# Batch 1 of a retention-then-MLP kernel: its last 256 tokens in 64-token chunks at two stops, its first 256 with 64-column states, and more half-width up products

## The chip, the cores and the metric

The kernel runs on one core of one Trainium2 chip. The metric is the device time of one execution in microseconds (us). A core has a matrix engine (TensorE, PE in the profile; its weight loads are PEld), a vector engine (DVE), a scalar engine (ACT), a general engine (POOL) and a queue engine (SP) that issues most transfers. Each runs its own list of instructions in order and waits on semaphores for the others.

## The reference

For 8 batches and 8 heads, with 576 tokens and 64 features a head, linear attention with a decay per head is computed; the heads are put side by side (512 features a token), and every one of the 4608 tokens goes through a two-layer network with a gate.

```python
scores = scale * np.matmul(q, k.transpose(0, 1, 3, 2))
gamma = 1.0 - 2.0 ** (-5.0 - np.arange(H, dtype=np.float32))
Dmat = np.where(rel >= 0, gamma[:, None, None] ** rel[None, :, :], 0.0)   # rel = query position - key position
ret = scores * Dmat[None, :, :, :]
attn_out = np.matmul(ret, v)
x = attn_out.transpose(0, 2, 1, 3).reshape(B * S, H * D)
h = x @ w_in                          # 512 -> 2048
g = h * (1.0 / (1.0 + np.exp(-beta * h)))
out = g @ w_out                       # 2048 -> 512
```

## The kernel before, in words

**Blocks.** The first 512 tokens of each batch are one block, and the last 64 tokens of all batches together are a ninth block. Each block is attended, which leaves a tile `xT` (features on partitions, tokens along the free axis); then 16 calls of `up` (one for each group of 128 hidden features: four matmuls over the 512 input features, and one ACT instruction that writes the gated result to `gT`) and 16 calls of `down` (four calls of four feature groups for each 128 tokens). Operands are bf16, sums are f32 in PSUM.

**Attention in chunks.** The decay is folded into q and v, so that a chunk needs a plain triangle mask. A chunk's output is (scores within the chunk) times v, plus q times a state, the running sum of the products of k and v over the earlier chunks. The kernel has three ways of doing it. Batch 0 uses functions with the prefix `s_`. Batch 1 uses four chunks of 128 tokens, numbered i = 4 to 7, each in these steps: `t_k` turns k with four transposes; `a_sc` makes scores and masks them on DVE; `a_st` adds the chunk's k by v to the state, as four 128x128 products of which only the two diagonal 64x64 blocks are of use, and copies these blocks to `sbds`; `a_O` multiplies the masked scores by v; `a_cross` adds q times the state (four products over the block-diagonal `sbds`); `a_x` copies the result to `xT`. `second(i)` runs `a_O`, `a_cross` and `a_x` for chunks i and i+1, and then `a_st(i + 1)`. Batches 2 to 7 use eight chunks of 64 tokens with 64x64 tiles of the array: `d_st(u, x)` makes the state products of four chunks and returns `chain`, which adds them up on DVE one after the other and copies each sum to bf16 in `sbq` (on ACT); `d_sc` makes scores and returns `masks` (two DVE instructions for each half); `d_out` makes outputs, first the products with v, then the products with the states in two passes, the second of which waits for a tiny DVE instruction, the fence; its `evict` copies four banks to `xT`. In these batches the heads in the second half of each tile are put in another order (`turned`, `head_of`), so that two products that run side by side write different banks.

**Order of work.** It is written out by hand. `fill` is the list of calls of `up` and `down` in order; `streams` holds the attention steps with keys, and `merged` puts a step before the entry of `fill` whose index reaches its key. `d0` is the index of block 0's first `down`, `u1` that of block 1's first `up`, and `base[m]` that of a later block, from which keys of later loads and attention steps are counted. Block 1's first ten feature groups are done in two halves of 256 tokens (`up(1, fo, 0, 2)`, then `up(1, fo, 2, 2)`), so that they can start on chunks 4 and 5 while chunks 6 and 7 are still attended. The steps of chunks 6 and 7 are spread between the half calls: `t_k(6)` ahead of the first one, `t_k(7)` behind it, and `a_sc(6)`, `a_sc(7)`, `a_st(6)` and `second(6)` further on, three half calls ahead of the second halves.

**PSUM.** There are eight banks: three with tag `mm`, two with `O`, two with `sc`, one with `st`. A new tile of a tag takes the oldest bank of that tag, and its first writer waits for the last reader of the old one.

Of the kernel before, what the change touches and what calls it, by code (L numbers as in the profile page):

```python
# [19 lines left out]
def kernel(  # L20
# [46 lines left out]
    NQ = 6  # L67
    E = CB
    XB = 2
    QB = 2  # L70
    HT = MB // 2
    VB = 4
    q_tiles, kv_tiles = {}, {}
# [208 lines left out]
    def pre_q(b, n):  # L282

        if n == 0:
            batch[b] = dict(qs=sb.tile([P, CB, H, D], BF16, name="qs", tag="qs", bufs=2),
                            qT=sb.tile([P, CB, HP, P], BF16, name="qT", tag="qT", bufs=2))
        if b < 2:
            hs, cs = slice(n // 2 * HP, (n // 2 + 1) * HP), slice(n % 2 * 2, n % 2 * 2 + 2)
            e = nc.vector
        else:  # L290
            if n % 2:
                return
            cs = slice(n, n + 2)
            for to, hs in turned:
                nc.gpsimd.tensor_tensor(batch[b]["qs"][:, cs, to], q_tiles[b][:, hs, cs].rearrange("p h i d -> p i h d"),  # L295
                                        gq[:, cs, hs].unsqueeze(3).to_broadcast([P, 2, len(range(H)[hs]), D]), ALU.mult)
            return
        e.tensor_tensor(batch[b]["qs"][:, cs, hs], q_tiles[b][:, hs, cs].rearrange("p h i d -> p i h d"),
                        gq[:, cs, hs].unsqueeze(3).to_broadcast([P, cs.stop - cs.start, hs.stop - hs.start, D]),
                        ALU.mult)  # L300

    def pre(i, js=(0, 1)):

# [57 lines left out]
    def q_cols(i, r, p):  # L361

        b, c = seq[i]
        if b is None:
            return live[i]["qkT"][r, 0, p, :], lambda o: o
        return (batch[b]["qT"][r, :, p, c * PC:(c + 1) * PC], lambda o: o.rearrange("k (i s) -> k i s", i=CB))
# [31 lines left out]
    def a_cross(i):  # L398

        b, c = seq[i]  # L400
        if c == 0:
            return
        for p in range(HP):
            rhs, view = q_cols(i, slice(0, P), p)
            nc.tensor.matmul(view(O_of(i, p)), sbds[c - 1][:, p, :], rhs, start=False, stop=True, skip_group_check=True)

    def a_O(i):

        b, c = seq[i]
        L = live[i]  # L410
        new_O(i)
        R, vn = L["R"], L["vn"]
        for j, p in [(n % 2, n // 2) for n in range(H)]:
            nc.tensor.matmul(O_of(i, p)[j * D:(j + 1) * D], vn[:, 2 * p + j, :], R[:, j, p, :],
                             start=opens(i, p), stop=c == 0, skip_group_check=True)

    def a_x(i):
# [9 lines left out]
    def a_st(i):  # L427

        b, c = seq[i]
        if b is None:  # L430
            return
        L = live[i]
        if c == 0:
            state_ps[b] = psum.tile([P, HP, P], F32, name="st", tag="st", bufs=1)
        st = state_ps[b]
        for p in range(HP):
            nc.tensor.matmul(st[:, p, :], heads(L["kn"], p), heads(L["vn"], p),
                             start=(c == 0 and p == 0), stop=True, skip_group_check=True)
        for j in range(2):
            r, cols = slice(j * D, (j + 1) * D), slice(j * D, (j + 1) * D)  # L440
            e = nc.vector.tensor_copy if i in (CB + 2, CB + 3) else nc.scalar.copy
            if c < CB - 1:
                e(sbds[c][r, :, cols], st[r, :, cols])
                continue
            e(ends[b][r, :2], st[r, :2, cols])
            e(ends[b][(1 - j) * D:(2 - j) * D, 2:], st[r, 2:, cols])

    spread = [(0, 0), (1, 1), (0, 1), (1, 0)]

# [104 lines left out]
    def after(later, earlier):  # L554
        tc.add_manual_dep(later.ins, earlier.ins.name, mybir.DependencyInfo(mybir.DependencyClass.Sync, mybir.DependencyReason.DATA))

    def d_sc(u):

        R = [sb.tile([P, 2, 2, HP, TL], BF16, name="R", tag="R", bufs=4) for _ in range(2)]
        sc = {}  # L560
        for x in range(2):
            for j in range(2):
                sc[x, j] = psum.tile([P, 2, HP, TL], F32, name="sc", tag="O" if x else "sc", bufs=2)
            for cl in range(2):
                for p in range(HP):
                    for j, hh in spread:
                        c = 4 * x + 2 * cl + hh
                        nc.tensor.matmul(columns(u, sc[x, j][half(hh), cl, p, :]), piece(u, c)["kT"][half(j), p, half(hh)],  # L568
                                         q_of(u, c, j, p), start=cl == 0 and p == 0, stop=True, skip_group_check=True)
        mask = tri[1 if u == B else 0][:].unsqueeze(1).to_broadcast([P, 2 * HP, TL])  # L570
        batch.setdefault(u, {})["R"] = R

        def masks(x):
            for j in range(2):
                nc.vector.tensor_tensor(R[x][:, j].rearrange("k c p q -> k (c p) q"),  # L575
                                        sc[x, j].rearrange("k c p q -> k (c p) q"), mask, ALU.mult)
        return masks

    def d_st(u, x):

        S = [psum.tile([P, 2, HP, D], F32, name="st", tag=t, bufs=n) for t, n in (("st", 1), ("mm", 3))]
        for cl in range(2):
            for p in range(HP):
                for hh, j in spread:
                    L = piece(u, 4 * x + 2 * cl + hh)
                    nc.tensor.matmul(S[hh][half(j), cl, p, :], L["kn"][half(hh), 2 * p + j, :],  # L586
                                     L["vn"][half(hh), head_of(u, p, j), :], start=cl == 0 and p == 0, stop=True,
                                     skip_group_check=True)

        def chain():  # L590
            for c in range(4 * x, 4 * x + 4):
                new, add = sums[c % 2], S[c % 2][:, c // 2 % 2]
                if c:
                    nc.vector.tensor_tensor(new[:], add, sums[(c - 1) % 2][:], ALU.add)  # L594
                else:
                    nc.vector.tensor_copy(new[:], add)
                nc.scalar.copy((sbq[c] if c < NC - 1 else ends[u])[:], new[:])  # L597
        return chain

    def d_out(u):  # L600
# [42 lines left out]
        return lambda: cross(1), evict  # L643


    gts = {}

    def up(m, fo, c0=0, cn=CB):
# [32 lines left out]
    def down(m, ms, f0, fn=4, n0=0, nn=d_model):  # L681

        gT = gts[m]
        if f0 == 0:
            pos_[ms] = psum.tile([P, d_model], F32, name="po", tag="mm" if m or ms < 3 else "st", bufs=3 if m or ms < 3 else 1)
        po = pos_[ms]
        for fo in range(f0, f0 + fn):
            parts = ((0, nn),) if m or fo < 5 else ((0, nn // 2), (nn // 2, nn))
            for x, y in parts:
                nc.tensor.matmul(po[:, x:y], gT[:, fo, ms, :], w_out_sb[:, fo, n0 + x:n0 + y],  # L690
                                 start=(fo == 0), stop=(fo == FO - 1), skip_group_check=m == 0)
        if f0 + fn < FO:
            return
        if m not in ots:
            ots[m] = stage.tile([P, MB // P, d_model], F32, name="ot", tag="wt", bufs=4)
        ot = ots[m][:, ms, n0:n0 + nn]
        (nc.scalar.copy if m == 0 else nc.vector.tensor_copy)(ot, po[:, :nn])  # L697
        if m < B:
            rows = out[m * S:m * S + MB].rearrange("(s i) n -> s i n", i=CB)
            if m < 2:  # L700
                held.append((rows[:, ms, n0:n0 + nn], ot))
            else:
                nc.sync.dma_start(rows[:, ms, n0:n0 + nn], ot)
        else:
            for x in range(2):
                r0 = (2 * ms + x) * S + MB
                nc.sync.dma_start(out[r0:r0 + TL, n0:n0 + nn], ot[x * TL:(x + 1) * TL])
# [102 lines left out]
    fill += [F(down_rows, n) for n in range(3)]  # L810
    fill += [F(down, 0, 3, 0)] + [F(down, 0, ms, f0) for f0 in (4, 8) for ms in range(4)] + [F(down, 0, ms, 12) for ms in (3, 0, 1, 2)]

    u1 = len(fill)
    fill += [F(up, 1, fo, 2 * x, 2) for x in range(2) for fo in range(10)]
    fill += [F(up, 1, fo) for fo in range(10, FO)]
    fill += [F(down, 1, ms, f0) for ms in range(MB // P) for f0 in range(0, FO, 4)]
    base = {1: u1 + 10}
    for n, m in enumerate(blocks[2:], 2):
        base[n] = len(fill)
        fill += [F(up, m, fo) for fo in range(FO)]  # L820
# [2 lines left out]
    fill += [F(down, blocks[-1], MB // P - 1, 0, FO, n0, nn) for n0, nn in ((0, 384), (384, 128))]  # L823

    def second(i):
        for f in (a_O, a_cross, a_x):
            f(i)
            f(i + 1)
        a_st(i + 1)

    def triangles():
        nc.gpsimd.memset(causal, 1.0)
# [2 lines left out]
        for t, pattern in zip(tri, ([[1, CB], [CB, TL // CB]], [[1, TL]])):  # L835
            nc.gpsimd.memset(t[:], 1.0)
            for x in range(2):
# [13 lines left out]
               [(d0 + 7, F(pre_q, 1, n)) for n in range(4)] + [(d0 + 12.5, F(pre_q, XB, n)) for n in range(4)] + [(d0 + 11.6, F(t_q, 1, 0)), (d0 + 12.6, F(t_q, 1, 1))],  # L851
               [(d0 + 8, F(pre, 4, (0,))), (d0 + 8, F(pre, 5, (0,))), (d0 + 9, F(pre, 4, (1,))), (d0 + 9, F(pre, 5, (1,))),
                (d0 + 12.7, F(t_k, 4)), (d0 + 14, F(t_k, 5)), (d0 + 14, F(a_sc, 4)), (d0 + 15, F(a_sc, 5)),
                (d0 + 15, F(a_st, 4)), (d0 + 15.9, F(second, 4))],
               [(d0 + 10, F(pre, 6, (0,))), (d0 + 10, F(pre, 7, (0,))), (d0 + 12, F(pre, 6, (1,))), (d0 + 12, F(pre, 7, (1,))),
                (d0 + 15.95, F(t_k, 6)), (u1 + 1, F(t_k, 7)), (u1 + 2, F(a_sc, 6)), (u1 + 3, F(a_sc, 7)),
                (u1 + 4, F(a_st, 6)), (u1 + 7, F(second, 6))]]


    def early_states(u):  # L860
# [85 lines left out]
```

## Time and profile before

| what | before |
|---|---|
| median of 3 runs, us | 297.1 (296.67 to 298.74) |
| the profiled execution, us | 297.28 |
| its span, first to last instruction, us | 295.5 |
| PE busy | 287.1 us, 97% of the span |
| ACT busy | 145.9 us, 49% |
| POOL busy | 111.1 us, 38% |
| DVE busy | 102.5 us, 35% |
| granted TensorE clock, mean | 1.000 |

The span is what the profile sees; 1.78 us of the profiled execution lie outside of it. Ends of matmuls are modelled, and a small share of matmul records is missing, so a count such as x27 may stand for 28. In the chain of work that ended last, PE has 96%. Block 1's attention lies between 42.2 and 55.5 us of the span; its `up` calls run from 49.5 to 66.4 us.

### The profile page before, as it was taken

To read this page: it belongs to the slowest core of one execution; us is meant where nothing else is said; L and a number is where in the kernel's file an instruction comes from. 1 tells how busy PE (TensorE), PEld (TensorE's weight loads), DVE (VectorE), ACT (ScalarE), POOL (GpSimd) and SP (SyncE) were. 2 spreads that over 40 slices of the span, in tenths; PEclk is the share of its full clock that TensorE was granted. 3 is DMA by queue.
4 is the path that set the end of the run, shared out by engine and by line. 5 is a ranking of instruction groups with operands and counts; after the bars stand their busy time and mean duration, and the time that the engine had idled before them with its cause. 6 is when DMAs were issued, how large, how long until landed. Compare 5 with 4: busy or idle time off the path is not lost.

```text
span 295.5 us, 7656 instructions
## 1 busy us (share of the span) xinstructions
PE 287.1 (97%) x3245; PEld 150.6 (51%) x3274; DVE 102.5 (35%) x213; ACT 145.9 (49%) x255; POOL 111.1 (38%) x219
## 2 busy tenths in 40 slices
PE   7999999999999999999999999999999999999995
PEld 3654587855544554445444544454554544444443
DVE  5764546604640551045204530354053500110012
ACT  5657537783278434843474347434780167007600
POOL 5957027955733713280438316754223000000000
PEclk9999999999999999999999999999999999999999
DMA  7999999999999898949999849998998110131011
GB/s 225 306 367 386 376 226 277 220 180 253 222 229 235 214 162 231 252 72 161 231 250 198 180 105 273 190 177 180 219 174 138 73 38 0 35 71 38 0 71 71
DMA packets 124033, 53.97 MB, mean 183 GB/s; under 512 B 101840, under 2 KB 116448, under 8 KB 124000
## 3 DMA queue, kind: packets, MB, share of 16 engines
q1 hardware_dynamic: 123968, 53.49, 82.1%
q8 instruction: 25, 0.41, 0.6%
q14 instruction: 8, 0.07, 0.1%
q10 hardware_dynamic: 32, 0.01, 0.0%
HBM read 36.71 MB, written 9.44 MB: 156 GB/s over the span
## 4 chain that ended last, share of the span: by engine, by line
PE 96%; DMA 1%; issue 1%; ACT 0%; DVE 0%; DVEq 0%
PE po L690 42%; PE ph L655 38%; PE ph L670 4%; PE O L614 2%; PE sc L568 1%; PE st L586 1%; DMA qn<-in_q_dram 1%; PE O L627 1%; PE T L352 1%; PE st L527 1%; PE sc L378 0%; PE sc L490 0%; PE O L504 0%; ACT kT L475 0%; PE ph L248 0%
## 5 line engine op out<-in xcount | busy, mean ns | idle before, releaser
L690 PE MATMUL po<-w_out_sb,gT 128*128 128x512 bf16 (+3 forms) x619 | 125.7, 358 | 2.3 <-issue 2.1
L657 ACT ACTIVATE gT<-ph,beta_sb 128x512 bf16<-128x512 f32 (+1 forms) x140 | 91.5, 659 | 50.9 <-PE ph L655 50.5
L655 PE MATMUL ph<-xT,w_in_sb 128*128 128x512 bf16 (+1 forms) x550 | 114.4, 364 | 0.5
L690 PEld LDWEIGHTS <-gT 128*128 128x128 bf16 x636 | 60.2, 98 | 60.7
L655 PEld LDWEIGHTS <-w_in_sb 128*128 128x128 bf16 x560 | 54.3, 98 | 57.5 <-DVE first L594 0.4
L697 DVE COPY ot<-po 128x512 f32<-128x512 f32 (+2 forms) x33 | 22.2, 672 | 72.2 <-PE po L690 69.4
L328 POOL CAST kn<-kvn 128x128 bf16<-128x128 f32 (+2 forms) x76 | 23.4, 343 | 46.1 <-DMA kvn<-in_k_dram 41.2
L295 POOL TENSOR_TENSOR qs<-qn,gq 128x256 bf16<-128x256 f32 (+1 forms) x36 | 26.3, 756 | 33.1 <-DMA qn<-in_q_dram 33.1
L575 DVE TENSOR_TENSOR R<-sc,tri 128x512 bf16<-128x512 f32 x28 | 17.4, 684 | 60.0 <-PE sc L568 60.0
L306 POOL TENSOR_TENSOR vn<-kvn,gv 128x512 bf16<-128x512 f32 x28 | 29.1, 1040 | 7.4 <-DMA kvn<-in_v_dram 7.1
L642 ACT CAST xT<-O 128x512 bf16<-128x512 f32 x14 | 7.5, 590 | 31.6 <-PE O L627 31.6
L597 ACT CAST sbd<-warm 128x256 bf16<-128x256 f32 x18 | 7.3, 407 | 25.6 <-DVE warm L594 20.6
L670 PE MATMUL ph<-xT,w_in_sb 128*128 128x512 bf16 x54 | 12.8, 379 | 0.1
L594 DVE TENSOR_TENSOR first<-st,warm 128x256 f32<-128x256 f32 x24 | 10.2, 425 | 2.9 <-ACT sbq L597 0.5
L316 POOL TENSOR_TENSOR kn<-tln,gq 128x128 bf16<-128x128 f32 (+1 forms) x12 | 5.6, 470 | 14.2 <-DMA tln<-in_q_dram 9.9
L594 DVE TENSOR_TENSOR warm<-st,first 128x256 f32<-128x256 f32 x18 | 7.6, 423 | 9.6 <-PE st L586 8.4
L673 ACT ACTIVATE gT<-ph,beta_sb 128x512 bf16<-128x512 f32 x14 | 8.7, 688 | 4.4 <-PE ph L670 4.4
L642 DVE CAST xT<-O 128x512 bf16<-128x512 f32 x14 | 9.0, 686 | 5.1 <-PE O L627 5.1
L214 POOL CAST w_in_sb<-wt 128x256 bf16<-128x256 f32 (+1 forms) x15 | 7.7, 530 | 5.0 <-DMA wt<-in_moe_w_in_dram 4.9
L597 ACT CAST sbd<-first 128x256 bf16<-128x256 f32 x18 | 7.3, 407 | 2.2 <-DVE first L594 0.2
L670 PEld LDWEIGHTS <-w_in_sb 128*128 128x128 bf16 x56 | 5.2, 97 | 6.3 <-issue 0.5
L231 DVE TENSOR_SCALAR w_out_sb<-wt,rbeta_sb 128x512 bf16<-128x512 f32 x13 | 5.9, 485 | 5.0 <-DMA wt<-in_moe_w_out_dram 5.0
(107 smaller groups left out, 166.1 us busy)
## 6 DMA issues: line engine op xcount, KB each, us to landing
qn<-in_q_dram SPq DMA_DIRECT2D x16, 512.0 KB, 5.2
kvn<-in_k_dram SPq DMA_DIRECT2D x32, 256.0 KB, 6.1
kvn<-in_v_dram SPq DMA_DIRECT2D x32, 256.0 KB, 5.1
out_dram<-ot SPq DMA_DIRECT2D x31, 256.0 KB, 3.4
wt<-in_moe_w_out_dram SPq DMA_DIRECT2D x8, 512.0 KB, 8.5
wt<-in_moe_w_in_dram SPq DMA_DIRECT2D x5, 512.0 KB, 8.8
wt<-in_moe_w_in_dram SPq DMA_DIRECT2D x6, 256.0 KB, 5.6
tln<-in_q_dram SPq DMA_DIRECT2D x8, 128.0 KB, 3.6
```

The lines of the kernel that those rows point to most:

```text
L295: nc.gpsimd.tensor_tensor(batch[b]["qs"][:, cs, to], q_tiles[b][:, hs, cs].rearrange("p h i d -> p i h d"), gq[:, cs, hs].unsqueeze(3).to_ ...
L306: nc.gpsimd.tensor_tensor(live[i]["vn"], kv_tiles.pop(i)[:, 1], gains(gv, c), ALU.mult)
L328: nc.gpsimd.tensor_copy(kn[:, c % 2, to], t[:, 0, hs])
L575: nc.vector.tensor_tensor(R[x][:, j].rearrange("k c p q -> k (c p) q"), sc[x, j].rearrange("k c p q -> k (c p) q"), mask, ALU.mult)
L594: nc.vector.tensor_tensor(new[:], add, sums[(c - 1) % 2][:], ALU.add)
L597: nc.scalar.copy((sbq[c] if c < NC - 1 else ends[u])[:], new[:])
L642: (nc.scalar.copy if n % 2 else nc.vector.tensor_copy)(x, o)
L655: nc.tensor.matmul(ph, w_in_sb[:, ko, fo * P:(fo + 1) * P], xts[m][:, ko, :, w], start=(ko == 0), stop=(ko == KO - 1))
L657: nc.scalar.activation(gts[m][:, fo, :, w], ph, ACT.Silu, scale=beta_sb[:, fo:fo + 1])
L670: nc.tensor.matmul(phs[f][:], w_in_sb[:, ko, f * P:(f + 1) * P], xts[m][:, ko], start=(ko == 0), stop=(ko == KO - 1))
L690: nc.tensor.matmul(po[:, x:y], gT[:, fo, ms, :], w_out_sb[:, fo, n0 + x:n0 + y], start=(fo == 0), stop=(fo == FO - 1), skip_group_check=m ...
L697: (nc.scalar.copy if m == 0 else nc.vector.tensor_copy)(ot, po[:, :nn])
```

## The change

It changes batch 1 alone.

- `QB = 1`: batch 1's heads now take the turned order of the later batches. Its `pre_q` makes two DVE instructions of 256 elements in place of one of 512 for the second half of the heads, and the cast of k on POOL is three instructions a chunk in place of one.
- Chunks 4 and 5 (the first 256 tokens) stay chunks of 128 tokens. `a_st` makes eight products 128x64 a chunk with 64 columns moving, in place of four 128x128; the new `a_keep` copies the state to `sbq` with one ACT instruction (and, behind chunk 5, to `sums` with one DVE instruction), in place of two ACT copies. `a_cross` makes eight 64x64 products in place of four. `second` puts `a_st(5)` ahead of `a_cross(5)`.
- Chunks 6 and 7 become four chunks of 64 tokens. `t_k(6)` and `t_k(7)` both stand ahead of the first half call. At the first stop, three half calls later, `late_scores` runs `d_st(1, 1)` and `d_sc` for one half, then on DVE the chain (two of its bf16 copies on DVE, one on ACT, the last sum written as bf16 at once) and behind it the two masks. At the second stop, seven half calls later, the new `half_out` makes products with v and with the states, and copies four banks to `xT` on DVE and ACT.
- Block 1's half-width `up` calls go from ten feature groups to thirteen. Its `down` calls of feature groups 10 to 15 make two matmuls of 256 columns in place of one of 512. Keys that hang on `base` move along with the three added entries.

```diff
-    QB = 2
+    QB = 1
...
     def a_cross(i):
         b, c = seq[i]
-        if c == 0:
-            return
         for p in range(HP):
-            rhs, view = q_cols(i, slice(0, P), p)
-            nc.tensor.matmul(view(O_of(i, p)), sbds[c - 1][:, p, :], rhs, start=False, stop=True, skip_group_check=True)
+            for j in range(2):
+                rhs, view = q_cols(i, half(j), p)
+                nc.tensor.matmul(view(O_of(i, p)[half(head_of(b, p, j) % 2)]), sbq[2 * c - 1][half(j), p, :], rhs,
+                                 start=False, stop=True, skip_group_check=True)
...
     def a_st(i):
...
         for p in range(HP):
-            nc.tensor.matmul(st[:, p, :], heads(L["kn"], p), heads(L["vn"], p),
-                             start=(c == 0 and p == 0), stop=True, skip_group_check=True)
-        for j in range(2):
...
+            for j in range(2):
+                nc.tensor.matmul(state_ps[b][half(j), p, :], L["kn"][:, 2 * p + j, :], L["vn"][:, head_of(b, p, j), :],
+                                 start=c == 0 and p == 0, stop=True, skip_group_check=True)
+
+    def a_keep(i):
+        b, c = seq[i]
+        nc.scalar.copy(sbq[2 * c + 1][:], state_ps[b][:])
+        if c:
+            nc.vector.tensor_copy(sums[c % 2][:], state_ps[b][:])
...
-        def chain():
-            for c in range(4 * x, 4 * x + 4):
-                new, add = sums[c % 2], S[c % 2][:, c // 2 % 2]
+        def chain(cs=range(4 * x, 4 * x + 4), e=nc.scalar.copy):
+            for c in cs:
+                new, add = sums[c % 2] if u != 1 or c < NC - 1 else ends[u], S[c % 2][:, c // 2 % 2]
...
-                nc.scalar.copy((sbq[c] if c < NC - 1 else ends[u])[:], new[:])
+                if new is not ends[u]:
+                    e((sbq[c] if c < NC - 1 else ends[u])[:], new[:])
...
+    def half_out(u):
+        O = {(hh, y): psum.tile([P, 2, CB, 2, TL // CB], F32, name="O", tag="sc" if y else "O", bufs=2)
+             for y in range(2) for hh in range(2)}
...
+        for other in range(2):
+            for n in range(16):
...
+                last = nc.tensor.matmul(to(CB + 2 * cl + hh, p, h % 2), piece(u, CB + 2 * cl)["vn"][half(hh), h, :],
+                                        columns(u, batch[u]["R"][1][half(hh), j, cl, p, :]),
+                                        start=(hh, y, h % 2) not in seen, stop=False, skip_group_check=True)
+                seen.add((hh, y, h % 2))
+            if not other:
+                fence = nc.vector.memset(fenced[:], 0.0)
+                after(fence, last)
+        for flip in range(2):
+            for n in range(16):
...
+                m = nc.tensor.matmul(to(c, p, j ^ y), sbq[c - 1][half(j), p, :], q_of(u, c, j, p),
+                                     start=False, stop=True, skip_group_check=True)
+                if flip and n < 2:
+                    after(m, fence)
+        for n, ((hh, y), o) in enumerate(O.items()):
+            x = xt(u)[:, 2 * y:2 * y + 2, :, MB // CB // 2:].rearrange("k p i (c h s) -> k (p i) c h s", c=2, h=2)
+            (dve, act)[n % 2](x[:, :, :, hh, :], o.rearrange("k p i c s -> k (p i) c s"))
...
-            parts = ((0, nn),) if m or fo < 5 else ((0, nn // 2), (nn // 2, nn))
+            parts = ((0, nn),) if m > 1 or fo < (10 if m else 5) else ((0, nn // 2), (nn // 2, nn))
...
-    u1 = len(fill)
-    fill += [F(up, 1, fo, 2 * x, 2) for x in range(2) for fo in range(10)]
-    fill += [F(up, 1, fo) for fo in range(10, FO)]
+    u1, NH = len(fill), 13
+    fill += [F(up, 1, fo, 2 * x, 2) for x in range(2) for fo in range(NH)]
+    fill += [F(up, 1, fo) for fo in range(NH, FO)]
...
-    base = {1: u1 + 10}
+    base = {1: u1 + NH}
...
     def second(i):
-        for f in (a_O, a_cross, a_x):
-            f(i)
-            f(i + 1)
+        a_O(i)
+        a_O(i + 1)
         a_st(i + 1)
+        a_cross(i + 1)
+        a_x(i)
+        a_x(i + 1)
+        a_keep(i + 1)
+
+    def late_scores():
+        chain, masks = d_st(1, 1), d_sc(1, (1,))
+        chain((4, 5), dve)
+        chain((6, 7))
+        masks(1)
...
-                (d0 + 15, F(a_st, 4)), (d0 + 15.9, F(second, 4))],
+                (d0 + 15, F(a_st, 4)), (d0 + 15, F(a_keep, 4)), (d0 + 15.9, F(second, 4))],
...
-                (d0 + 15.95, F(t_k, 6)), (u1 + 1, F(t_k, 7)), (u1 + 2, F(a_sc, 6)), (u1 + 3, F(a_sc, 7)),
-                (u1 + 4, F(a_st, 6)), (u1 + 7, F(second, 6))]]
+                (d0 + 15.95, F(t_k, 6)), (d0 + 15.96, F(t_k, 7)), (u1 + 3, late_scores), (u1 + 10, F(half_out, 1))]]
```

More of the change, by code (lines that the diff above doesn't have):

```diff
@@ L288, in pre_q @@
             hs, cs = slice(n // 2 * HP, (n // 2 + 1) * HP), slice(n % 2 * 2, n % 2 * 2 + 2)
-            e = nc.vector
+            for to, hs in [(hs, hs)] if n < 2 or b < QB else turned[1:]:
+                nc.vector.tensor_tensor(batch[b]["qs"][:, cs, to], q_tiles[b][:, hs, cs].rearrange("p h i d -> p i h d"),
+                                        gq[:, cs, hs].unsqueeze(3).to_broadcast([P, 2, len(range(H)[hs]), D]), ALU.mult)
         else:
@@ L296, in pre_q @@
                                         gq[:, cs, hs].unsqueeze(3).to_broadcast([P, 2, len(range(H)[hs]), D]), ALU.mult)
-            return
-        e.tensor_tensor(batch[b]["qs"][:, cs, hs], q_tiles[b][:, hs, cs].rearrange("p h i d -> p i h d"),
-                        gq[:, cs, hs].unsqueeze(3).to_broadcast([P, cs.stop - cs.start, hs.stop - hs.start, D]),
-                        ALU.mult)
     def pre(i, js=(0, 1)):
@@ L400, in a_cross @@
         b, c = seq[i]
-        if c == 0:
-            return
         for p in range(HP):
-            rhs, view = q_cols(i, slice(0, P), p)
-            nc.tensor.matmul(view(O_of(i, p)), sbds[c - 1][:, p, :], rhs, start=False, stop=True, skip_group_check=True)
+            for j in range(2):
+                rhs, view = q_cols(i, half(j), p)
+                nc.tensor.matmul(view(O_of(i, p)[half(head_of(b, p, j) % 2)]), sbq[2 * c - 1][half(j), p, :], rhs,
+                                 start=False, stop=True, skip_group_check=True)
     def a_O(i):
@@ L413, in a_O @@
         for j, p in [(n % 2, n // 2) for n in range(H)]:
-            nc.tensor.matmul(O_of(i, p)[j * D:(j + 1) * D], vn[:, 2 * p + j, :], R[:, j, p, :],
+            h = head_of(b, p, j)
+            nc.tensor.matmul(O_of(i, p)[half(h % 2)], vn[:, h, :], R[:, j, p, :],
                              start=opens(i, p), stop=c == 0, skip_group_check=True)
@@ L429, in a_st @@
         b, c = seq[i]
-        if b is None:
-            return
         L = live[i]
         if c == 0:
-            state_ps[b] = psum.tile([P, HP, P], F32, name="st", tag="st", bufs=1)
-        st = state_ps[b]
+            state_ps[b] = psum.tile([P, HP, D], F32, name="st", tag="st", bufs=1)
         for p in range(HP):
-            nc.tensor.matmul(st[:, p, :], heads(L["kn"], p), heads(L["vn"], p),
-                             start=(c == 0 and p == 0), stop=True, skip_group_check=True)
-        for j in range(2):
[L440 to L446, printed above, removed]
+            for j in range(2):
[6 more added lines that the diff above has]
+            nc.vector.tensor_copy(sums[c % 2][:], state_ps[b][:])
     spread = [(0, 0), (1, 1), (0, 1), (1, 0)]
@@ L555, in after, with d_sc @@
         tc.add_manual_dep(later.ins, earlier.ins.name, mybir.DependencyInfo(mybir.DependencyClass.Sync, mybir.DependencyReason.DATA))
-    def d_sc(u):
-        R = [sb.tile([P, 2, 2, HP, TL], BF16, name="R", tag="R", bufs=4) for _ in range(2)]
+    def d_sc(u, xs=(0, 1)):
+        R = {x: sb.tile([P, 2, 2, HP, TL], BF16, name="R", tag="R", bufs=4) for x in xs}
         sc = {}
-        for x in range(2):
+        for x in xs:
             for j in range(2):
-                sc[x, j] = psum.tile([P, 2, HP, TL], F32, name="sc", tag="O" if x else "sc", bufs=2)
+                sc[x, j] = psum.tile([P, 2, HP, TL], F32, name="sc", tag="O" if x and u != 1 else "sc", bufs=2)
             for cl in range(2):
@@ L579, in d_st @@
     def d_st(u, x):
-        S = [psum.tile([P, 2, HP, D], F32, name="st", tag=t, bufs=n) for t, n in (("st", 1), ("mm", 3))]
+        S = [psum.tile([P, 2, HP, D], F32, name="st", tag=t, bufs=n) for t, n in (("st", 1), ("O", 2) if u == 1 else ("mm", 3))]
         for cl in range(2):
@@ L643, in d_out, with to @@
         return lambda: cross(1), evict
+    def half_out(u):
+        O = {(hh, y): psum.tile([P, 2, CB, 2, TL // CB], F32, name="O", tag="sc" if y else "O", bufs=2)
+             for y in range(2) for hh in range(2)}
+        seen = set()
+        def to(c, p, x):
+            return O[c % 2, p // 2][half(x), p % 2, :, c // 2 % 2]
+        for other in range(2):
+            for n in range(16):
+                cl, pp, y, hh = n // 8, n // 4 % 2, n // 2 % 2, n % 2
+                p, j = pp + 2 * y, hh if other else 1 - hh
+                h = head_of(u, p, j)
+                last = nc.tensor.matmul(to(CB + 2 * cl + hh, p, h % 2), piece(u, CB + 2 * cl)["vn"][half(hh), h, :],
[7 more added lines that the diff above has]
+            for n in range(16):
+                cl, pp, y, j = n // 8, n // 4 % 2, n // 2 % 2, n % 2
+                c, p = CB + 2 * cl + (j ^ flip), pp + 2 * y
+                m = nc.tensor.matmul(to(c, p, j ^ y), sbq[c - 1][half(j), p, :], q_of(u, c, j, p),
[5 more added lines that the diff above has]
+            (dve, act)[n % 2](x[:, :, :, hh, :], o.rearrange("k p i c s -> k (p i) c s"))
     gts = {}
@@ L687, in down @@
         for fo in range(f0, f0 + fn):
-            parts = ((0, nn),) if m or fo < 5 else ((0, nn // 2), (nn // 2, nn))
+            parts = ((0, nn),) if m > 1 or fo < (10 if m else 5) else ((0, nn // 2), (nn // 2, nn))
             for x, y in parts:
                 nc.tensor.matmul(po[:, x:y], gT[:, fo, ms, :], w_out_sb[:, fo, n0 + x:n0 + y],
-                                 start=(fo == 0), stop=(fo == FO - 1), skip_group_check=m == 0)
+                                 start=(fo == 0), stop=(fo == FO - 1), skip_group_check=m < 2)
         if f0 + fn < FO:
```

## The prediction

> **What bounds the kernel now.** I read the page first: the busy shares, then the 40 slices. A slice is 7.39 us.
>
> ```profile
> PE 287.1 (97%) x3245; PEld 150.6 (51%) x3274; DVE 102.5 (35%) x213; ACT 145.9 (49%) x255; POOL 111.1 (38%) x219
> ...
> PE   7999999999999999999999999999999999999995
> ...
> PEclk9999999999999999999999999999999999999999
> ```
>
> PE is at 9 in all but the first and the last slice. No engine, no queue and no clock holds it up for long, so the change is worth what it adds to or takes from PE's own list, plus any wait it creates. Next I read the chain of waits in order of time around batch 1's attention (start us, us, what).
>
> ```profile
> 46.64 0.33 PE sc L378 x8
> 46.97 0.33 PE st L437 x4
> 47.30 0.87 PE po L690 x8
> 48.17 0.59 PE O L414 x16
> 48.76 0.33 PE O L405 x4
> 49.09 0.22 PE st L437 x4
> 49.31 0.22 PE T L358 x4
> 49.53 0.57 PE ph L655 x4
> 50.11 0.22 PE T L358 x4
> 50.33 0.44 PE ph L655 x4
> 50.77 0.46 PE sc L378 x8
> ...
> 54.18 0.57 PE O L414 x16
> 54.74 0.55 PE O L405 x8
> 55.30 0.22 PE st L437 x4
> ```
>
> Nothing but PE stands in it. Four 128x128 products take 0.22 us by themselves and 0.33 behind a tile of another shape, so a switch of shape costs 0.11. The first half group takes 0.57 where the next takes 0.44: 0.13 of it is a wait for `xT`. From 50.33 to 55.52 are 5.19 us; six half groups in it, at 4 x 107.9 ns, are 2.59, which leaves 2.60 us to chunks 6 and 7.
>
> The prices of the new form come from the same view where batch 2 is attended.
>
> ```profile
> 72.04 0.38 PE st L586 x32
> 72.41 0.58 PE sc L568 x64
> 73.00 0.16 issue
> ...
> 79.14 0.64 PE O L614 x58
> 79.79 0.26 PE O L627 x25
> 80.05 0.40 PE st L586 x32
> 80.45 0.24 PE O L627 x25
> 80.69 0.16 issue
> ```
>
> A 64x64 product of 64 columns costs 9 to 12 ns, four tiles at once, and going back to full tiles 0.16 us.
>
> **First half, chunks 4 and 5.** Eight 128x64 products of 64 columns replace four 128x128 (0.22). The trace has no such product. Below: half of the array at a time, so four times 27 ns, 0.11. Above: `a_O`'s pace on the same tiles, 0.57/16 = 36 ns, with twice the columns, so 0.29. I take 0.17, near the lower end, since weight loads of small tiles keep up with 12 ns above. For `a_st(4)` a way back from half tiles to full ones (0.11) is new: 0.33 becomes 0.28 + 0.11, which is +0.06. For `a_st(5)`: -0.05, and it needs no switch behind `a_O`. The eight cross products, two at a time over 128 columns, cost 0.21 + 0.11, as now (0.33); from 64x64 back to the transposes 0.13 is new, between 0.11 and 0.16. Sum: +0.14.
>
> Then a wait moves. `t_k(7)` now directly follows `t_k(6)`, and its bank is the `sc` bank that ACT empties in `a_x(5)`. That copy ran from 49.17 to 49.56 now. It would start at 49.38, when the later cross products are done, and end at 49.77, so `t_k(7)` starts at about 49.83, while `t_k(6)` ends at 49.67: 0.16 of wait. Queued behind it are all half groups, and the first of them then finds `xT` ready, so its own 0.13 goes away: +0.03. First half: **+0.17**, from -0.15 (0.11 for the states, crosses at 0.21, no wait) to +0.45 (0.29, crosses at 0.35, 0.3 of wait).
>
> **Second half, chunks 6 and 7.** The first stop is 32 state products (0.38), 32 score products (half of 0.58, 0.29) and the way back (0.16): 0.83. The second is 32 products with v (half of 0.64), 32 cross products at 0.50/56 each (0.29), 0.06 to enter and 0.16 to leave: 0.83. Against 2.60 this is **-0.94**, from -1.1 (no entry cost and half of the ways back) to -0.8 (entries at 0.11 twice).
>
> **The wait that can take it back.** `half_out` starts with products on the masked scores, and DVE reaches the masks only behind the chain. The costs are in the list of DVE's instructions after batch 2's scores (start us, us, what), and in the groups kept apart by shape.
>
> ```profile
> 72.83 2.48 DVE L575 TENSOR_TENSOR R<-sc,tri 128x512 bf16<-128x512 f32 x4 [1.79 <-PE sc L568]
> 75.23 0.41 DVE L594 TENSOR_TENSOR warm<-st,first 128x256 f32<-128x256 f32 x1
> 75.75 0.42 DVE L594 TENSOR_TENSOR first<-st,warm 128x256 f32<-128x256 f32 x1
> 76.28 0.42 DVE L594 TENSOR_TENSOR warm<-st,first 128x256 f32<-128x256 f32 x1
> ```
> ```profile
> L216 DVE CAST w_in_sb<-wt 128x256 bf16<-128x256 f32 x5 | 1.6, 343 | 1.2 <-DMA wt<-in_moe_w_in_dram 1.2
> ```
>
> One add follows the last at 0.53, though it lasts 0.42; masks run at 0.62 each. The new order is add, copy, add, copy, add, add, mask, mask. A copy from SBUF to bf16 is nearest to the 0.343 cast, 0.29 where the next instruction doesn't need it: 4 adds at 0.53, 2 copies at 0.29, less 0.14 behind the last add, which the masks don't need, then 0.62 + 0.68 for the masks: 3.86. DVE starts 0.06 behind the state products. PE reaches the first stop at 50.5 + 2 x 0.43 = 51.36, finishes the states at 51.74, so DVE runs from 51.80 to 55.66 and PE may go on at 55.72. PE itself is at the second stop after scores and way back (52.19) and seven half groups (3.02): 55.21. **Wait: +0.51**. Below: 0, if the copies cost next to nothing and the adds hide. Above: 1.2, if both copies hold up their successors at 0.53 and the masks start after a full gap. If this cover is gone altogether, the second halves wait too, since they need `xT`. The fence and the second cross pass are hidden behind 16 products and the first pass (0.31).
>
> **Half groups and half downs.** Three feature groups become 24 matmuls of 256 columns for 12 of 512. Block 0's stretch with halves runs at 107.9 ns (5.18 us for 48), a full one elsewhere at 213.9 (5.99 for 28): 1.9 ns a pair, so 12 x 1.9 = 0.02, and 24 pairs in `down` 0.05. ACT needs 0.44 for a half group against PE's 0.43, so 6 more of them cost up to 0.06 if ACT paces them. I take **+0.11**, from 0 to +0.25.
>
> **At nothing.** POOL's casts of k grow from 0.61 to 0.87 us for each of four chunks (the three-instruction form is in the trace at 0.87). The list of POOL's instructions shows it idle for 0.2 to 0.8 us, waiting for transfers, around these chunks; k of chunk 7 is done at 47.74 for a transpose at 49.8, v of chunk 7 at 50.22 for the states at 51.36. With that slack of 1.1 us gone, every us goes to the first stop. DVE's two smaller gain instructions add about 0.3 us to an end at 41.42, before transposes at 43.56. ACT: `a_keep` is 0.41 for 0.76, twice; one chain copy and two copies to `xT` (0.41 each) are new, under PE's 1.66 us of attention. No transfer is added, and no step of SP's list changes places: the steps keyed to `base` keep their order in the lists of SP and POOL, which run ahead of PE.
>
> **The sum** against the profiled execution (span 295.5, time 297.28): 0.17 - 0.94 + 0.51 + 0.11 = -0.15, so a span of 295.35 and a time of 297.13. That execution is 0.18 above the median of the runs shown (297.1), so the median comes to **296.9 us**. All low ends together give -1.25 (295.8), all high ends +1.1 (298.2).
>
> **Rivals.**
> (1) *The chain is hidden.* Without the wait the sum is -0.66: 296.4. For it: adds that wait for nothing could close up from 0.53 to 0.42, which alone gives back 0.4. Against it: in every later batch they stand 0.53 apart.
> (2) *Slower: DVE sets the second stop.* One mechanism, at the masks: each of the six chained links takes 0.53 and DVE starts late, because v of chunk 7 comes late from its transfer (POOL waited 0.61 us for that pair now). From 1.1 us of wait on, the change loses; at 1.6, with half a us from a late v, it is +0.95: 298.0. Against it: the 1.1 us of slack.
> (3) *ACT paces the half groups.* 26 at 0.44 and 1.23 of new copies are 12.7 us against PE's 11.2 + 1.66 + 0.5 = 13.4 in the same stretch. At the isolated 0.476 a group it would be 13.6, and the three `mm` banks would pass 0.2 to 0.4 on: 297.2.
> (4) *The small products don't run side by side.* At the full tiles' pace 64 columns cost 27.5 ns (half of 0.22/4), so the 128 products of the two stops would be 3.52 us in place of 1.28: +2.2, 299.1. The rows above speak against it at more than twice the pace. [...]
> (5) *It doesn't do what it says*, because work ahead of 42 us or a transfer decides: PE's 97% leave no room.
>
> **Chances.** Forecast 0.48, (1) 0.27, (2) 0.12, (3) 0.07, (4) 0.03, (5) and unseen stalls 0.03. Range: the bounds of the terms and rival (2), **295.8 to 298.2**; rival (4) is left out. About 1%, 3 us, is what a measurement of this kernel can tell from no change. No term can gain 3 us, since chunks 6 and 7 hold 2.6 in all: faster 0.02. Slower by 3 us takes (4) with a wait on top, or an unseen stall: 0.04. Within 1%: 0.94.
>
> **What would show it.** Right: PE's chain has about 1.66 us at the two stops in place of 2.60, a gap of about 0.5 us ahead of the first product with v, put down to DVE's masks, and a shorter one ahead of `t_k(7)`, put down to ACT's copy to `xT`; from the first full `up` of block 1 on, all is the same and shifted by under 0.3 us. Wrong: products of the stops at 20 ns or more, a gap at the first stop put down to POOL, gaps between half groups put down to ACT, or a shift that grows in later blocks.

## The result, and the profile after

The changed kernel is **slower by a little**: 297.72 us median (296.89 to 300.13, 22 runs) against 297.10 before (296.51 to 298.74, 22 runs), ratio 1.0025 with a 95% interval of 1.0014 to 1.0036. Forecast were 296.9 and a small gain; the time lies inside the range and the band of 1%, but on the other side of no change. The profiled execution took 297.72 us, its span is 296.0 us, 0.5 longer than before.

The page's busy shares are those of before to within one per cent of the span (PE 97%, ACT 49%, POOL 38%, DVE 34%) and tell nothing of the loss. The chain of waits in order of time (start us, us, what), at the same place as before, does:

```profile
46.88 0.24 PE st L434 x8
...
48.73 0.49 ACT xT L424
49.22 0.29 ACT xT L422
...
49.55 0.38 PE T L356 x4
49.93 1.31 PE ph L686 x12
51.24 0.44 PE st L582 x32
51.68 0.42 DVE warm L590
...
53.61 0.41 ACT sbq L594
54.01 0.38 ACT gT L688
...
54.44 1.91 PE ph L686 x16
56.34 0.38 PE O L657 x32
```

Before, only PE stood in this stretch. Now the chain leaves PE twice. The first time, ahead of `t_k(7)` (L356), was forecast. The second runs from the state products (L582) over DVE's adds and copies (L590, and L594 with `sbd`) to ACT's copy of one state (`sbq`, L594), then to a gated result of a half group (`gT`, L688), and only then back to PE. In the lists of PE, ACT and DVE (start us, us, engine, line and operation, in brackets the idle time before it and what ended it):

```profile
54.44 1.91 PE L686 MATMUL ph<-xT,w_in_sb 128*128 128x256 bf16 x16 [1.11 <-ACT gT L688]
```
```profile
53.61 0.41 ACT L594 CAST sbq<-warm 128x256 bf16<-128x256 f32 x1 [1.85 <-DVE warm L590]
53.92 2.94 ACT L688 ACTIVATE gT<-ph,beta_sb 128x256 bf16<-128x256 f32 x7
```
```profile
53.95 1.28 DVE L571 TENSOR_TENSOR R<-sc,tri 128x512 bf16<-128x512 f32 x2
```

ACT did nothing for 1.85 us. It had come to the copy of the chain's third sum and waited for DVE's third add; the gated results of the half groups stand behind the copy in its list. PE filled the three `mm` banks with three half groups and then stood for 1.11 us. At the second stop, where the wait was expected, there was none: the two masks (L571) were done at 55.23, and PE came there at 56.3, late already.

### The profile page after: what moved, and what is told of

Its sections match the earlier page's. It is cut to its first block, busy times and chain, and to the rows that moved or that the text cites. A ratio compares the mean times of both kernels' runs of the same rounds, so it can differ in the third digit from the quotient of the medians.

```text
span 296.0 us, 7954 instructions
## 1 busy us (share of the span) xinstructions
PE 288.3 (97%) x3402; PEld 152.6 (52%) x3402; DVE 101.6 (34%) x215; ACT 146.1 (49%) x259; POOL 112.3 (38%) x227
## 4 chain that ended last, share of the span: by engine, by line
PE 93%; DMA 2%; POOL 1%; ACT 1%; DVE 1%; SPq 1%; issue 0%
PE po L721 43%; PE ph L686 38%; PE ph L701 4%; DMA kvn<-in_k_dram 2%; PE st L582 2%; PE O L611 2%; PE O L624 1%; PE sc L564 1%; PE st L523 1%; POOL kn L463 1%; PE O L500 0%; SPq L104 0%; POOL vn L463 0%; SPq L84 0%; PE O L508 0%; PE T L350 0%
## 5 line engine op out<-in xcount | busy, mean ns | idle before, releaser
L721 PE MATMUL po<-w_out_sb,gT 128*128 128x512 bf16 (+3 forms) x660 | 128.9, 352 | 0.0
L688 ACT ACTIVATE gT<-ph,beta_sb 128x512 bf16<-128x512 f32 (+1 forms) x143 | 91.5, 649 | 48.8 <-PE ph L686 48.6
L721 PEld LDWEIGHTS <-gT 128*128 128x128 bf16 x660 | 62.6, 98 | 58.7
L686 PEld LDWEIGHTS <-w_in_sb 128*128 128x128 bf16 x572 | 55.6, 98 | 57.2 <-issue 1.5
L326 POOL CAST kn<-kvn 128x128 bf16<-128x128 f32 (+1 forms) x84 | 24.6, 334 | 44.2 <-DMA kvn<-in_k_dram 44.1
L571 DVE TENSOR_TENSOR R<-sc,tri 128x512 bf16<-128x512 f32 x30 | 18.6, 682 | 60.0 <-PE sc L564 60.0
L594 ACT CAST sbd<-warm 128x256 bf16<-128x256 f32 x18 | 7.3, 405 | 25.3 <-DVE warm L590 20.5
L590 DVE TENSOR_TENSOR warm<-st,first 128x256 f32<-128x256 f32 x20 | 8.4, 421 | 10.4 <-PE st L582 9.2
L590 DVE TENSOR_TENSOR first<-st,warm 128x256 f32<-128x256 f32 x25 | 10.6, 425 | 2.5
L701 PEld LDWEIGHTS <-w_in_sb 128*128 128x128 bf16 x56 | 5.2, 98 | 6.2 <-POOL w_in_sb L214 0.5
L594 ACT CAST sbd<-first 128x256 bf16<-128x256 f32 x18 | 7.3, 405 | 2.3 <-DVE first L590 0.3
```

Source lines behind the costliest of these rows:

```text
L326: nc.gpsimd.tensor_copy(kn[:, c % 2, to], t[:, 0, hs])
L594: e((sbq[c] if c < NC - 1 else ends[u])[:], new[:])
L686: nc.tensor.matmul(ph, w_in_sb[:, ko, fo * P:(fo + 1) * P], xts[m][:, ko, :, w], start=(ko == 0), stop=(ko == KO - 1))
L688: nc.scalar.activation(gts[m][:, fo, :, w], ph, ACT.Silu, scale=beta_sb[:, fo:fo + 1])
L701: nc.tensor.matmul(phs[f][:], w_in_sb[:, ko, f * P:(f + 1) * P], xts[m][:, ko], start=(ko == 0), stop=(ko == KO - 1))
```

## Experiments

The ratios below are to the kernel before, from runs on the same chip.

### The copy that holds ACT

**e1_copy_on_dve.**

```diff
-        chain((6, 7))
+        chain((6, 7), dve)
```

> The changed kernel with the chain's third bf16 copy (state 6) on DVE too, in place of ACT. Theory A, ACT's queue is held: ACT meets that copy in order, waits 1.85 us for DVE's third add, and the gated results of the half groups behind it wait too, until the three mm banks are full. Then PE's wait of 1.11 us between half groups goes; DVE's masks end some 0.3 us later (about 55.5), so 0.3 to 0.4 us of wait appear at the second stop; time about 0.75 us under the changed kernel, 0.1 under the kernel before. Theory B, ACT has too much work: 0.41 us less on ACT take 0.4 us off the wait, 0.4 off the time. Theory C, DVE's chain and masks set the second stop: 0.3 us longer than the changed kernel.

Measured: 297.32 us, ratio 0.9995 (0.9978 to 1.0012). The wait between half groups is gone, and one at the second stop has come, 0.8 us where 0.3 to 0.4 was expected:

```profile
PE O L657 <- DVE R L571: 0.8, 1, 0.8
```

The copy itself took 0.68 us on DVE here, not 0.29 (why, no run shows), and the masks ended at 55.93. Theory A's sign and place are right, the new wait was undersized. Theory C alone would have made this kernel slower than the changed one; against the kernel before, the changed one stands at 1.0025 (1.0014 to 1.0036), above this interval.

**e2_copy_later.** The same copy, on ACT, behind four more half groups.

```diff
-        chain((6, 7))
+        chain((6, 7), None)
...
-                if new is not ends[u]:
+                if new is not ends[u] and e:
...
-(u1 + 10, F(half_out, 1))
+(u1 + 7, F(act, sbq[6][:], sums[0][:])), (u1 + 10, F(half_out, 1))
```

> The changed kernel with the same copy on ACT, but issued four half groups later (ahead of the call at u1 + 7), when DVE's third add is done; nothing else changes on any engine. Theory A (ACT's queue held by an early wait): the wait of 1.11 us goes to 0, the masks still end about 55.2, under 0.2 us of wait at the second stop; time about 1.0 us under the changed kernel, 0.4 under the kernel before (ratio 0.9985). Theory B (too much work on ACT): ACT's work is the same, so the wait stays near 1.1 us and the time the same. Theory C (DVE sets the second stop): the same time.

Measured: 296.89 us, ratio 0.9981 (0.9967 to 0.9995), faster than the kernel before; theory A had 0.9985. No engine does more or less than in the changed kernel; one ACT instruction has moved down its list. The chain of waits:

```profile
52.18 1.87 PE ph L686 x16
...
54.07 1.29 DVE R L571 x2
...
55.40 0.44 PE O L657 x32
```

PE's seven half groups run without a break. The list of PE's waits between 36 and 90 us has one entry, that ahead of `t_k(7)`:

```profile
PE T L356 <- ACT xT L422: 0.2, 1, 0.2
```

DVE's masks still end last ahead of the second stop, but PE loses under 0.2 us to them. This rules out too much work on ACT (theory B): its work is the same, and the wait is gone.

**e4_copies_on_act.**

```diff
-        chain((4, 5), dve)
+        chain((4, 5))
```

> The changed kernel with the chain's first two bf16 copies moved from DVE to ACT, so that all three are there. Theory A (ACT is held until DVE's third add, not loaded): the add ends 0.4 us sooner, as no copy stands ahead of it on DVE (53.15 for 53.57); the two copies on ACT fall into its idle time; the wait goes from 1.11 to about 0.7 us and the time is 0.4 us under the changed kernel. Theory B (too much work on ACT): 0.82 us more on ACT, the wait grows to about 1.9 us, time 0.8 us over the changed kernel.

Measured: 297.53 us, ratio 1.0002 (0.9986 to 1.0017); the wait is

```profile
PE ph L686 <- ACT gT L688: 0.7, 1, 0.7
```

as theory A had it; the ratio is 0.7 us under that of the changed kernel, where 0.4 was expected and the intervals allow both. With 0.82 us more work on ACT, PE waits 0.4 us less, because the add that ACT waits for comes sooner. It is the wait, not the load.

### How much cover DVE's chain needs

**e8_ten_half_groups.** On top of e2_copy_later:

```diff
-    u1, NH = len(fill), 13
+    u1, NH = len(fill), 10
...
-(u1 + 10, F(half_out, 1))
+(u1 + 7, F(half_out, 1))
...
```

> e2_copy_later with ten half-width feature groups in place of thirteen and the second stop three half groups earlier (ahead of the call at u1 + 7, the late copy right before it), so that four half groups, not seven, stand between the stops. By the theory that DVE's chain and masks end 3.5 us behind the state products whatever PE does, PE is at the second stop three half groups (1.3 us) sooner and waits for the masks: about 1.5 us of wait where e2_copy_later has 0.2, time 1.3 us over e2_copy_later, 0.7 us over the kernel before (ratio 1.0025). Rival: the half groups' number is of no account, DVE or ACT run sooner too, and the time is that of e2_copy_later.

Measured: 298.37 us, ratio 1.0040 (1.0021 to 1.0059): 1.2 us over the kernel before, by the interval 0.6 to 1.8, where 0.7 was expected. The wait is the one that was expected:

```profile
PE O L657 <- DVE R L571: 1.5, 1, 1.5
```

DVE needs 3.5 us from the state products to the masks (51.73 to 55.26) here, as in the changed kernel (51.67 to 55.23), though PE is at the second stop at 53.8 here and at 56.3 there. The score products and seven half groups of 0.43 us between the stops cover it almost exactly, with four half groups they do not.

### The half-width calls by themselves

**e3_halves_alone.** On the kernel before:

```diff
-    u1 = len(fill)
-    fill += [F(up, 1, fo, 2 * x, 2) for x in range(2) for fo in range(10)]
-    fill += [F(up, 1, fo) for fo in range(10, FO)]
+    u1, NH = len(fill), 13
+    fill += [F(up, 1, fo, 2 * x, 2) for x in range(2) for fo in range(NH)]
+    fill += [F(up, 1, fo) for fo in range(NH, FO)]
...
-    base = {1: u1 + 10}
+    base = {1: u1 + NH}
...
-            parts = ((0, nn),) if m or fo < 5 else ((0, nn // 2), (nn // 2, nn))
+            parts = ((0, nn),) if m > 1 or fo < (10 if m else 5) else ((0, nn // 2), (nn // 2, nn))
...
```

> The kernel before with only the thirteen half-width feature groups and the half-width down calls of block 1 (keys moved along). By the prediction's terms +0.11 us: 0.02 to 0.08 in the up calls, 0.05 in the down calls, 297.2. Rival: these edits carry most of the 0.6 us that the changed kernel is slower, +0.4 us or more, in block 1's down calls or as waits of PE for ACT between half groups.

Measured: 299.08 us, ratio 1.0047 (1.0031 to 1.0063): +1.4 us, far over the 0.11. The rival had its size and named block 1's down calls, but it isn't spread over them: the `up` calls behind the attention take 10.89 us for 10.86 before, and the loss is one hole, late in the down calls, shown in the chain of waits:

```profile
80.87 1.73 PE po L690 x9
82.60 1.56 issue
84.16 1.16 PE po L690 x9
```

"Issue" is time in which PE waited for nothing that the profile shows. (Pieces of it of 0.05 and 0.16 us in the kernel before are of another kind: its profile has 3245 product records for 3274 loads; from 20 us of the span on, the chain of the changed kernel, with 3402 for 3402, has none over 0.04 us, and this one's none over 0.02 but the hole.) Ahead of the hole lie a dense stretch of small products, the 152 of a batch's outputs and the next batch's first states (79.30 to 80.87), and 1.73 us of down calls. What PE stood for, no record shows. The rows that the texts below count are entries of PE's list, a load and a product for each of 3274 before, so 6548; this kernel has 72 more. The changed kernel has the same half-width calls and no such hole, so they are not what made it slower.

**e5_half_ups_alone** has only the `NH` and `base` lines of that diff, **e6_half_downs_alone** only the `parts` line, and **e9_more_half_downs** has that line with a 4 in place of the 10.

> The kernel before with only the thirteen half-width feature groups (24 more rows in PE's list). e3_halves_alone lost 1.4 us where 0.11 was expected, in one gap of 1.56 us of PE in block 1's last down calls, with nothing waited for. [...] Theory G, the half-width calls themselves cost the time: +0.7 us here, the other part in e6_half_downs_alone.

> The kernel before with only the half-width down calls of block 1 (48 more rows). [...] Theory G: the loss is spread over the 48 half-width matmuls, 0.7 us or more, with no gap.

> The kernel before with block 1's down calls in halves from feature group 4 on (48 pairs, 96 more rows). [...] Theory G: twice the loss of e6_half_downs_alone, spread over block 1's down calls, and later batches as before.

Measured: e5 297.51 us, ratio 1.0010 (0.9996 to 1.0023); e6 297.40 us, ratio 0.9997 (0.9985 to 1.0010); e9 301.98 us, ratio 1.0148 (1.0128 to 1.0168). The first two have no hole: no piece of PE's time with nothing waited for is over 0.2 us there. Each half of the edit costs next to nothing, and both together 1.4 us: costs of single calls (theory G) can't do that. e9 has a hole in batch 2 and one in batch 3, and none in batch 4:

```profile
81.61 1.54 issue
...
112.83 1.12 issue
```

Like that of e3, both holes come behind a stretch of 152 small products, the first 0.43 us behind its end (81.18), the second 3.1 us (109.71). Behind the same stretch in batch 4 there is none. So the holes don't go with the half-width calls one by one: none with 12 products more in PE's list (e5) and with 24 (e6), one with 36 (e3), two with 48 (e9), and none in the changed kernel, whose list has 128 more (3402 for 3274). No record names a cause. The two holes of e9's profile make 2.7 us of the 4.4 that its runs lost. The profiled run is the shortest, 300.62 us; the other four took 301.87 to 302.07, some 1.4 us more, and no profile shows where.

**e7_late_copy_full_downs.** e2_copy_later with the `parts` line as before.

> e2_copy_later without the half-width down calls (48 rows fewer). By the cost of a pair of halves (1.9 ns, 24 pairs) 0.05 us faster than e2_copy_later. [...]

Measured: 296.78 us, ratio 0.9984 (0.9970 to 0.9999), and no hole (its longest piece with nothing waited for is 0.2 us, with 104 products more in PE's list than the kernel before). Block 1's down stage and the attention in it take 16.91 us (65.71 to 82.62) where e2_copy_later took 16.96 (65.92 to 82.88): the 0.05 us of the forecast. It and e2_copy_later can't be told apart by their runs; both beat both kernels.

## Why the prediction was wrong

**What failed is one step: the line "At nothing ... ACT".** It weighed ACT's new instructions by their length (three of 0.41 us under PE's 1.66 us of attention), and didn't ask what stands behind each of them in ACT's list while it waits. The chain's third sum comes 1.9 us after the state products; its copy was written ahead of the gated results of seven half groups. A wait of 1.85 us on an engine that is busy 49% of the time became 1.11 us on the one that is busy 97%. The prediction had the right chain and DVE times that were nearly right, but followed them to the masks alone, and not to the other reader of the same sums. Rival (3), ACT as a pace-setter, named the engine and the `mm` banks, but by its load; e4 shows that the load isn't it. The prediction's own list of what would show it wrong has "gaps between half groups put down to ACT", and that is what came.

**The wait at the second stop**, +0.51, was nil in the changed kernel, because PE came late, and under 0.2 us in e2_copy_later. The term was too large by 0.3 to 0.5: DVE's chain and masks took 3.56 us (51.67 to 55.23), not 3.86. Link by link, an add with its copy took 0.67 and 0.82 us where 0.82 was written for each, the last two adds together 0.79 for 0.92, the masks 1.28 for 1.30. Its kind was right: e8 shows 1.5 us once three half groups of cover are gone. One more slip is in rival (2): by the prediction's own sum the change loses from 0.66 us of wait on, not from 1.1.

**The first half**, +0.17, was right. From the score products' end to the end of the first half group 3.36 us became 3.49 (46.88 to 50.37, the first half group put at 0.44): +0.13. The eight 128x64 products with their switch took 0.24 us where 0.28 was written, and the wait ahead of `t_k(7)` 0.18 where 0.16 was.

**The second half**, -0.94, was right. The starts in the changed kernel's list of PE give the price of each stop, once the half groups ahead of it are taken off at the prediction's 107.9 ns a product:

```profile
49.77 1.47 PE L686 MATMUL ph<-xT,w_in_sb 128*128 128x256 bf16 x12
...
51.84 1.48 PE L686 MATMUL ph<-xT,w_in_sb 128*128 128x256 bf16 x12
...
57.05 1.70 PE L686 MATMUL ph<-xT,w_in_sb 128*128 128x256 bf16 x14
```

From 49.77 to 51.84 are 2.07 us, 12 products take 1.30, which leaves 0.77 to the first stop; from 54.44 to 57.05 are 2.61, 16 products take 1.73, which leaves 0.88 to the second. Together 1.65 where 1.66 was forecast, against 2.60 before. So the new form does save what it was said to, and four small products side by side cost what batch 2's rows said (32 products with v in 0.38 us): rival (4) doesn't hold here.

**Half groups and half downs**, +0.11, were about right in place: the two profiles show +0.02 us in the `up` calls (e5: 10.88 for 10.86) and +0.05 to +0.09 in block 1's down stage (e2 against e7; e6's 17.10 for 17.01 before). What the prediction left out is that the same calls can come with a hole: on the kernel before they did (1.56 us in e3), in the changed kernel they did not, and no run shows why.

**The sum by what was measured.** The wait between half groups costs more than its 1.11 us of idle time. The products overlap (the 12 from 51.84 on start 0.11 us apart, and the last ends at 53.32), and the idle time counts from that end. By starts, 2.60 us pass from 51.84 to 54.44 for 12 products that need 1.30, so 1.30 is lost. With it the sum is 0.13 - 0.95 + 1.30 + 0.1 = +0.58, near the 0.5 us between the two spans and the 0.62 us between the medians. With the 1.30 taken out and under 0.2 put in for the masks it is about -0.6, and e2_copy_later's median is 0.46 under the kernel before. That 297.72 still lies in the forecast range is luck: a loss of 1.30 that was in no term was partly made up for by the forecast wait of 0.51 that didn't come.

**Open**: what PE stood for in the holes of e3 and e9; why the changed kernel, with e3's half-width calls, has none; and why e9's other runs lost more than its profile shows.

## What to carry to other kernels

When a step puts an instruction on an engine that isn't the bottleneck, ask in whose list it stands, what it waits for, and what stands behind it: here one early wait held ACT, busy 49% of the time, for 1.85 us, and once the three banks between them were full PE stood for 1.11 us. Moving that one copy four calls down its list turned a loss of 0.25% into a gain of 0.19%. Price a chain on a side engine to every reader of its results, not only to the last.

## What the runs showed that was not expected

PE stood still with no engine, semaphore or transfer of data named as the cause: for 1.56 us in e3, for 1.54 and 1.12 us in e9. Each time this came 0.4 to 3.1 us behind a dense stretch of 152 small products, which PE is through in 1.5 to 1.6 us; behind the same stretch in batch 2 of the kernel before, of the changed kernel, e5, e6 and e7 there was no such hole. So edits that each cost nothing (e5, e6) cost 1.4 us together (e3), and the only sign was a long piece of "issue" time in PE's chain. Why, no run shows.
